# Attention scores of the last 64 rows of every head: made during the first batch, stored in DRAM and loaded again where their top 32 are searched

## The chip, the cores and the metric

One core of a Trainium2 chip runs the whole kernel. The metric is device time in microseconds (us) of one execution. Before the change three runs took 1207.24, 1211.10 and 1211.47 us, median 1211.1. The five engines of the core each work through their own list of instructions in order and wait for one another by semaphores: PE multiplies matrices, DVE (VectorE) searches the largest scores, ACT (ScalarE) copies and exponentiates, POOL (GpSimd) subtracts and scales, and SP issues all DMA transfers.

## The reference

Sparse attention and then two feed-forward layers (FFN), all in float32:

```python
B, H, S, D = 4, 8, 576, 64                      # q, k, v: (B, H, S, D)
scores = matmul(q, k^T) / sqrt(D)               # 576 x 576 for each of the 32 heads
kth    = the 32nd largest score of each row
attn   = softmax over the scores >= kth, 0 elsewhere
x      = matmul(attn, v)                        # heads side by side: 2304 tokens x 512
h = x @ moe_w_in;   x = max(0.01 * h, h) @ moe_w_out            # 512 -> 2048 -> 512
h = x @ moe2_w_in;  g = h where h >= 1, 0 where h <= -1, (h + 1)^2 / 4 between
out = g @ moe2_w_out
```

## The kernel before

**Units.** A head has 576 rows of queries, which is 4 x 128 + 64. The attention is cut into 80 units. A unit of kind "m" is 256 rows of one head: two tiles of 128 rows x 576 scores. There are 16 of them in each batch. A unit of kind "r" takes the last 64 rows of two neighbouring heads and stacks them into one tile of 128 rows, so that there are 4 in each batch and 16 in all. The r units do not run with their own batch: those of batches 0, 1 and 2 stand in batch 2 (`REMS`, line 32), and those of batch 3 in batch 3. So batch 0 and batch 1 have 16 units each, batch 2 has 28 and batch 3 has 20.

**A unit's path.** `st_scores` (line 720) loads the head's keys and queries and multiplies them on PE (`scores`, line 544). Except in the first eight heads ("plain", float32 products), every product is made of two float32r products: ACT casts the keys and the queries, POOL makes the remainders (`k_new`, `q_new`). Half a tile (288 columns) is made at a time, and ACT copies it from PSUM into a tile `s`, of which there are six. `topk` (line 571) then searches the 32 largest of each row on DVE with four MAX8 and three MATCH_REPLACE8 a tile, ACT and POOL make the probabilities `e`, PE transposes them and multiplies them with V (`pv`, `pv_pair`), and `split_x` makes the operands of the FFN.

**An r unit before.** It loads its queries from `qp`, where two heads' queries stand in columns of their own with zeros in the others', casts them, and takes both heads' keys. Where its batch is the one that runs, the keys are there already; otherwise both are loaded and split again. That is so in 8 of the 16 r units. Each half tile is then the sum of four float32r products (two heads x two parts), so an r unit has eight.

**The FFN.** A table (`FLOW`, line 36) says which blocks of rows go through which layer together. Its matmuls (`hidden`, `sums`, lines 818 to 873) have 512 columns, or 256 for the first rows of batch 0. Each product is again three float32r matmuls (lines 795 to 797, and 867 to 869). The weights come packed and are decoded once (`prep_w`, line 431: two operations of ACT, one of POOL and one of DVE, and a split by ACT and POOL), 64 tiles in all, during batches 0 and 1; they are written to DRAM (`scr`) and loaded later into six `ring` buffers. The FFN of batch 0 starts inside batch 0, with the weight tiles `px` as they come.

**What sets the order.** A planner (`Plan`, line 76) writes the instructions of all engines once, ahead of time, from assumed durations and a priority for each operation (the unit's number for attention, over 10000 for the FFN). What it has written is each engine's program; on the chip nothing overtakes. So PE's program is one fixed interleaving of attention and FFN, and SP's is one list of all the transfers.

## Time and profile before

| | |
|---|---|
| three runs | 1207.24, 1211.10, 1211.47 us |
| span of the profiled execution, first to last instruction | 1207.4 us |
| busy in it: PE, DVE, ACT, POOL | 1149.2, 876.4, 856.5, 742.6 us |
| bytes read from and written to DRAM | 187.5 and 38.3 MB |

The profiled execution's own time is not listed beside its span; a span of 1207.4 us puts it at the lower end of the three runs, 3.7 us (0.3%) under their median. A profile's busy time of PE counts each matmul with its way through the array, while the next already runs: a matmul of 512 columns shows 0.39 us though the next starts 0.23 us after it. So PE at 100% means that there was always one on its way, and how fast PE works is read from the starts of successive matmuls. PEclk is the granted TensorE clock as a share of 2.4 GHz; its two levels are 1.2 and 2.4 GHz.

### The profile page before, as it was taken

How to read it: one execution, taken by the hardware profiler on the slowest of the kernel's cores; microseconds unless marked ns; L12 is line 12 of the kernel's file. 1: busy time of each engine (PE TensorE's matmuls, PEld its weight loads, DVE VectorE, ACT ScalarE, POOL GpSimd, SP SyncE). 2: the span in 40 equal slices, each digit the busy share in tenths (PEclk: the TensorE clock that was granted, in tenths of full speed). 3: DMA queues.
4: the chain of work that ended last, by engine and by line, in shares of the span. 5: the costliest groups of instructions: out<-in, count | busy, mean ns of one | idle time of the engine just before them, and what ended most of it. 6: DMA issues, size and time to landing. Idle time of an engine off the chain costs nothing.

```text
span 1207.4 us, 18958 instructions
## 1 busy us (share of the span) xinstructions
PE 1149.2 (95%) x6304; PEld 979.6 (81%) x6304; DVE 876.4 (73%) x1759; ACT 856.5 (71%) x1921; POOL 742.6 (62%) x852
## 2 busy tenths in 40 slices
PE   5678987999999999999999999999999999999998
PEld 4457976998888888888888888888888888888886
DVE  7999999999999995998999999989981000012221
ACT  6788998998999898799989898987553211242222
POOL 2445786985988779697969578868563222242221
PEclk9788998999999999999999999999999999999999
DMA  9655985797557456655556454433445432333323
GB/s 318 201 193 192 352 323 185 254 349 274 207 215 250 171 178 197 204 184 185 184 194 225 160 194 151 140 128 122 140 157 178 154 130 99 121 140 140 127 103 103
DMA packets 71410, 227.02 MB, mean 188 GB/s; under 512 B 7952, under 2 KB 14224, under 8 KB 67216
## 3 DMA queue, kind: packets, MB, share of 16 engines
q1 hardware_dynamic: 71312, 225.80, 53.8%
q8 instruction: 50, 0.82, 0.3%
q14 instruction: 48, 0.39, 0.1%
HBM read 187.50 MB, written 38.27 MB: 187 GB/s over the span
## 4 chain that ended last, share of the span: by engine, by line
PE 79%; ACT 8%; POOL 5%; DVE 5%; issue 2%; DMA 1%; SPq 0%; POOLq 0%; ACTq 0%; DVEq 0%
PE bank L795 14%; PE bank L797 14%; PE bank L796 14%; PE bank L660 7%; PE bank L634 6%; PE bank L557 6%; PE bank L867 5%; PE bank L869 5%; PE bank L868 5%; DVE wk L584 2%; DVE m L580 2%; ACT e L602 2%; PE bank L680 2%; POOL px L381 1%; POOL e L619 1%
## 5 line engine op out<-in xcount | busy, mean ns | idle before, releaser
L381 POOL TENSOR_TENSOR gt<-gr,gt 128x512 fp32r<-128x512 f32 x144 | 189.0, 1313 | 235.2 <-ACT gt L365 115.6
L580 DVE MAX8 m<-wk 128x8 f32<-128x576 f32 x432 | 309.9, 747 | 1.1
L843 DVE TENSOR_SCALAR t<-bank 128x512 f32<-128x512 f32 x72 | 49.5, 687 | 240.0 <-PE bank L797 239.3
L584 DVE MATCH_REPLACE8 wk<-m,wk 128x576 f32<-128x576 f32 x288 | 212.4, 742 | 0.0
L795 PE MATMUL bank<-x,ring 128*128 128x512 f32 (+1 forms) x568 | 208.9, 368 | 0.2 <-DVE gr L846 0.2
L797 PE MATMUL bank<-x,ring 128*128 128x512 f32 (+1 forms) x568 | 203.3, 358 | 0.0
L796 PE MATMUL bank<-x,ring 128*128 128x512 f32 (+1 forms) x568 | 202.9, 357 | 0.0
L634 PE MATMUL bank<-idt,e 128*116 128x128 f32 (+1 forms) x720 | 114.4, 287 | 30.0 <-POOL e L619 26.0
L634 PEld LDWEIGHTS bank<-idt,e 128*116 128x116 f32 (+1 forms) x720 | 88.6, 141 | 52.5 <-POOL e L619 33.8
L580 DVE MAX8 m<-s 128x8 f32<-128x576 f32 x144 | 104.3, 746 | 31.4 <-ACT s L365 31.2
L365 ACT COPY s<-bank 128x288 f32<-128x288 f32 x288 | 106.5, 402 | 28.4 <-PE bank L557 27.0
L365 ACT COPY ptr<-bank 116x512 f32<-116x512 f32 (+1 forms) x224 | 107.3, 508 | 26.5 <-PE bank L634 25.7
L381 POOL TENSOR_TENSOR pt<-ptr,pt 116x512 fp32r<-116x512 f32 (+1 forms) x96 | 106.1, 1124 | 30.2 <-ACT pt L365 28.4
L797 PEld LDWEIGHTS bank<-x,ring 128*128 128x128 f32 x568 | 106.6, 188 | 17.4
L619 POOL TENSOR_SCALAR e<-e,rc 128x576 f32<-128x576 f32 x144 | 109.8, 772 | 16.5 <-DVE rc L617 14.4
L367 ACT ACTIVATE t<-t,half 128x512 f32<-128x512 f32 x72 | 52.0, 722 | 93.8 <-DVE t L843 93.7
L367 ACT ACTIVATE gt<-bank 128x512 fp32r<-128x512 f32 x72 | 43.2, 601 | 105.6 <-PE bank L797 105.4
L795 PEld LDWEIGHTS bank<-x,ring 128*128 128x128 f32 x568 | 106.9, 188 | 12.2 <-DVE gr L846 0.7
L796 PEld LDWEIGHTS bank<-x,ring 128*128 128x128 f32 x568 | 107.1, 189 | 11.2 <-POOL x L381 0.4
L795 PE MATMUL bank<-gt,ring 128*128 128x512 f32 (+1 forms) x304 | 110.4, 363 | 0.0
L367 ACT ACTIVATE e<-s,nb 128x576 f32<-128x576 f32 x144 | 108.9, 779 | 1.4
L557 PE MATMUL bank<-kk,qh 128*128 128x288 f32 x512 | 104.3, 310 | 4.3 <-ACT s L365 2.9
(92 smaller groups left out, 2875.6 us busy)
## 6 DMA issues: line engine op xcount, KB each, us to landing
ring<-scr SPq DMA_DIRECT2D x212, 512.0 KB, 3.5
scr<-px SPq DMA_DIRECT2D x58, 512.0 KB, 4.2
wraw<-in_moe_w_in_dram SPq DMA_DIRECT2D x16, 1024.0 KB, 6.1
wraw<-in_moe_w_out_dram SPq DMA_DIRECT2D x16, 1024.0 KB, 6.8
kraw<-in_km_dram SPq DMA_DIRECT2D x56, 288.0 KB, 3.9
vl<-in_vd_dram SPq DMA_DIRECT2D x24, 320.0 KB, 4.5
qraw<-in_qm_dram SPq DMA_DIRECT2D x24, 256.0 KB, 4.1
vl<-in_vp_dram SPq DMA_DIRECT2D x16, 320.0 KB, 3.8
```

Of the source, the lines that this page charges most:

```text
L365: nc.scalar.copy(out=out_(), in_=in_())
L367: nc.scalar.activation(out=out_(), in_=in_(), func=func, **a)
L381: lambda: nc.gpsimd.tensor_tensor(out=out_(), in0=in0(), in1=in1(), op=ALU.subtract),
L557: nc.tensor.matmul(ps()[:, 0:HALF], lhsT=qh()[:, at] if plain else qh()[:, part, at], rhs=kk()[:, c * HALF:(c + 1) * HALF], start=(i == 0) ...
L580: vec(lambda i=i, c=c, src=src: nc.vector.max(out=m()[:, i, c], in_=src()), 664, [(m, (i, r))], [src], pr)
L584: vec(lambda i=i, c=c, src=src, w=ws[i]: nc.vector.match_replace(out=w(), in_to_replace=m()[:, i, c], in_values=src(), imm_value=NEG), 720 ...
L619: P.op("P", T_NORM, lambda i=i: nc.gpsimd.tensor_scalar(out=es[i](), in0=es[i](), scalar1=rc()[:, i:i + 1], scalar2=1.0, op0=ALU.mult, op1 ...
L634: nc.tensor.transpose(ps()[0:p, i * 128:(i + 1) * 128], e()[:, cols[j]], idt())
L660: nc.tensor.matmul(out_ps()[:, 0:w], lhsT=vt()[0:p, j, :], rhs=pt()[0:p, c] if lean else pt()[0:p, part, c], start=bi == 0 and part == 0 a ...
L795: nc.tensor.matmul(ps, lhsT=wh, rhs=xh, start=first, stop=False, skip_group_check=True)
L796: nc.tensor.matmul(ps, lhsT=wh, rhs=xl, start=False, stop=False, skip_group_check=True)
L797: nc.tensor.matmul(ps, lhsT=wl, rhs=xh, start=False, stop=last, skip_group_check=True)
```

## The change

The scores of the r units are no longer made where they are used. During the first 16 units (batch 0), after each unit's own scores, `scores_kept` makes those of one r unit, in the order of `KEPT`: head pair 0 of batches 0 to 3, then head pair 1, and so on. The host lays out a new array `kp`: for each pair of heads and each half of the keys, 128 partitions that hold the first head's 64 dimensions above the second head's, with 288 columns of keys and behind them 128 columns of queries, where each head's 64 queries have zeros in the other head's partitions. One float32 product of 288 columns, contracted over all 128 partitions, is then a finished half tile for both heads. For each half there is a load of 208 KB, that product, a copy by ACT into a tile `t` and a store of 144 KB to DRAM. The loads go into buffers `gr` and `wa`, in turn. An r unit now only loads its 288 KB of scores into an `s` tile (`scores_again`) and its V. In the planner, the buffer for such a load has to be free for 2500 ns (`SLACK`) before the load is placed.

```diff
@@ -57,6 +57,9 @@
 NLEAN = 16
 NPLAIN = 8
 NSOFT = 72
+KEPT = tuple((b, c) for c in range(4) for b in (0, 1, 2, 3))
+HOMES = ("gr", "wa")
+PKEPT = (1.0, 1.0)
 FREE = (8.0, 14.0)
 
 
@@ -91,7 +94,7 @@
 
     def tile(self, tag, make, fifo=True, among=None):
         r = Ref(tag, make)
-        r.seq, r.fifo, r.among = None, tag if fifo is True else fifo, among
+        r.seq, r.fifo, r.among, r.loaded = None, tag if fifo is True else fifo, among, False
         return r
 
     def op(self, eng, ns, fn, w=(), r=(), prio=0.0, after=(), also=()):
@@ -149,6 +152,8 @@
             if ref.fifo and given.get(ref.fifo, 0) != ref.seq:
                 return None
             free = slots[ref.tag]
+            if ref.loaded:
+                free = {i: t + SLACK for i, t in free.items()}
             can = [i for i in (ref.among or free) if free.get(i, 1e18) <= now]
             return min(can, key=free.get) if can else None
 
@@ -230,8 +235,9 @@
                     if uses[ref] == 0 and ref.tag in self.bufs:
                         hop = HOP + (SLACK if ref.tag in LOADED else 0.0)
                         slots[ref.tag][ref.slot] = now + hop
-                        heapq.heappush(events, (now + hop, cnt, -1))
-                        cnt += 1
+                        for late in (0.0, SLACK):
+                            heapq.heappush(events, (now + hop + late, cnt, -1))
+                            cnt += 1
                 for j in succ[i]:
                     left[j] -= 1
                     e2 = self.ops[j][0]
@@ -279,8 +285,8 @@
     ctx: ExitStack,
     tc: tile.TileContext,
     qm: bass.AP,
-    qp: bass.AP,
     km: bass.AP,
+    kp: bass.AP,
     vm: bass.AP,
     vd: bass.AP,
     vp: bass.AP,
@@ -568,6 +574,31 @@
                 [(s, c)], [ps], pr)
         return s
 
+    def scores_kept(b, c, j, pr):
+
+        d = fixed([128, S], F32, f"s{b}_{c}", lambda: dram)
+        kept[b, c] = d
+        n = HALF + 2 * REM
+        for z in range(2):
+            kq = new(HOMES[j % len(HOMES)], [128, 512], fifo="keptk")
+            dma(lambda kq=kq, z=z: kq()[:, 0:n], lambda z=z: kp[b, c, z], n / 2, [kq], [], pr)
+            ps = bank(pr)
+            s = new("t", [128, 512], fifo="kept")
+            pe(lambda kq=kq, ps=ps: nc.tensor.matmul(
+                ps()[:, 0:HALF], lhsT=kq()[:, HALF:n], rhs=kq()[:, 0:HALF], start=True, stop=True),
+                4 * HALF / 2.4, [ps], [kq], pr, [s])
+            act(lambda s=s: s()[:, 0:HALF], lambda ps=ps: ps()[:, 0:HALF], t_a(HALF, True), [s], [ps], pr)
+            dma(lambda z=z: d()[:, z * HALF:(z + 1) * HALF], lambda s=s: s()[:, 0:HALF], 144, [(d, z)], [s], pr)
+
+    def scores_again(b, c, pr):
+
+        s = new("s", [128, S])
+        s.loaded = True
+        dma(s, kept[b, c], 288, [s], [kept[b, c]], pr)
+        return s
+
+    kept = {}
+
     def topk(tiles, soft, scale, pr):
 
         n = len(tiles)
@@ -732,10 +763,7 @@
             t0 = 2 * a if b in JOINT else 0
             return dict(u=u, tiles=[scores([(qh, t0 + t, kk)], pr, plain) for t in range(2)], v=vt,
                         scale=scale / 2 if plain else scale)
-        ks = [k_cur[b, 2 * h + e] if b == u_batch[0] else k_new(b, 2 * h + e, pr) for e in range(2)]
-        vt = v_pair(b, h, pr)
-        qh = q_new(lambda: qp[b, h], T, pr)
-        return dict(u=u, tiles=[scores([(qh, e, ks[e]) for e in range(2)], pr)], scale=scale, v=vt)
+        return dict(u=u, tiles=[scores_again(b, h, pr)], scale=scale, v=v_pair(b, h, pr))
 
     def second():
 
@@ -975,6 +1003,8 @@
             if i == 0:
                 made.add(0)
                 prep_layer(0)
+            if i < len(KEPT):
+                scores_kept(*KEPT[i], i, PKEPT[0] + PKEPT[1] * i)
             st[i]["es"] = topk(st[i]["tiles"], i < NSOFT, st[i]["scale"], float(i))
         if i >= AHEAD:
             unit_out(i - AHEAD)
@@ -999,13 +1029,14 @@
         return np.concatenate([a, a], axis=2)
 
     data.append(("qm", twice(q[:, :, :QM])))
-    qp = np.zeros((B, H // 2, 2 * D, 4 * REM), q.dtype)
-    last = twice(q[:, :, QM:])
+    data.append(("km", twice(k)))
+    half = S // 2
+    kp = np.zeros((B, H // 2, 2, 2 * D, half + 2 * REM), q.dtype)
     for e in range(2):
-        o = e * 128 + e * REM
-        qp[..., o:o + REM] = last[:, e::2]
-    data.append(("qp", qp))
-    data.append(("km", twice(k)))
+        kp[:, :, :, e * D:(e + 1) * D, :half] = k[:, e::2].reshape(B, H // 2, 2, half, D).transpose(0, 1, 2, 4, 3)
+        at = half + e * REM
+        kp[:, :, :, e * D:(e + 1) * D, at:at + REM] = q[:, e::2, None, QM:].transpose(0, 1, 2, 4, 3)
+    data.append(("kp", kp))
     nj = -(-S // KB)
     vp = np.zeros((B, H, nj * KB, D), v.dtype)
     vp[:, :, :S] = v
```

Names in the following rows: `kraw`, `qraw`, `vl`, `vraw` are loaded keys, queries and V; `wraw` is a packed weight; `idt` is the identity; `gr` and `wa` in the changed program hold the loaded `kp`; `bank` is PSUM; `s`, `t` and `x` are as above, and `s<number>_<number>` is the DRAM array of one kept r unit.

SP's list at the start of the program. Before, from the second packed weight on:

```order
L359 DMA wraw_151<-in_moe_w_in_dram 128x2048
L359 DMA vl_153<-in_vd_dram 128x640
L359 DMA kraw_155<-in_km_dram 128x576
L359 DMA qraw_157<-in_qm_dram 128x256
L359 DMA vl_161<-in_vd_dram 128x640
L359 DMA kraw_165<-in_km_dram 128x576
L359 DMA qraw_171<-in_qm_dram 128x256
```

Now, from the same transfer on:

```order
L365 DMA wraw_151<-in_moe_w_in_dram 128x2048
L365 DMA vl_153<-in_vd_dram 128x640
L365 DMA gr_155<-in_kp_dram 128x416
L365 DMA gr_157<-in_kp_dram 128x416
L365 DMA kraw_161<-in_km_dram 128x576
L365 DMA qraw_165<-in_qm_dram 128x256
L365 DMA vl_171<-in_vd_dram 128x640
L365 DMA wa_174<-in_kp_dram 128x416
L365 DMA wa_182<-in_kp_dram 128x416
L365 DMA kraw_187<-in_km_dram 128x576
L365 DMA qraw_189<-in_qm_dram 128x256
```

Two loads of `kp` now stand ahead of the second unit's keys and queries, and two more ahead of the third's.

PE's list behind the transposes of the tenth unit. Before (`L660` is the product with V, `L557` the next scores, `L795` and the two after it the FFN's hidden products):

```order
L660 MATMUL bank_222<-ptr_299,vl_161 128x256 x2
L660 MATMUL bank_222<-ptr_304,vl_161 128x256 x2
L660 MATMUL bank_222<-ptr_311,vl_161 128x256
L557 MATMUL bank_228<-kraw_155,qraw_157 128x288
L557 MATMUL bank_176<-kraw_155,qraw_157 128x288
L795 MATMUL bank_214<-x_437,ring_965 128x256
L796 MATMUL bank_214<-x_437,ring_965 128x256
L797 MATMUL bank_214<-x_437,ring_965 128x256
```

Now, at the same place (`L691` is the product with V, `L563` the scores, `L587` a kept product, `L665` the next unit's transposes):

```order
L691 MATMUL bank_169<-ptr_325,vl_171 128x256 x2
L691 MATMUL bank_169<-ptr_334,vl_171 128x256 x2
L691 MATMUL bank_169<-ptr_337,vl_171 128x256
L563 MATMUL bank_236<-kraw_161,qraw_165 128x288
L563 MATMUL bank_176<-kraw_161,qraw_165 128x288
L563 MATMUL bank_239<-kraw_161,qraw_165 128x288
L563 MATMUL bank_169<-kraw_161,qraw_165 128x288
L587 MATMUL bank_236<-wa_174 128x288
L665 MATMUL bank_176<-idt,e_252 116x128
```

A kept product stands between the scores and the next transposes, and the FFN's products that stood here come later in the list.

SP's list in batch 2, at a run of r units. Before:

```order
L359 DMA kraw_165<-in_km_dram 128x576
L359 DMA qraw_157<-in_qp_dram 128x256
L359 DMA ring_781<-scr0_5_1_1078 128x1024
L359 DMA ring_850<-scr0_8_0_908 128x1024
L359 DMA kraw_137<-in_km_dram 128x576
L359 DMA ring_965<-scr0_6_1_1204 128x1024
L359 DMA qraw_171<-in_qp_dram 128x256
```

Now, at the first run of them:

```order
L365 DMA ring_963<-scr0_5_0_574 128x1024
L365 DMA vraw_4238<-in_vm_dram 128x320
L365 DMA s_167<-s2_0_386 128x576
L365 DMA s_180<-s0_0_247 128x576
L365 DMA ring_1074<-scr0_3_1_921 128x1024
L365 DMA ring_702<-scr0_6_0_755 128x1024
L365 DMA vraw_4245<-in_vm_dram 128x320
L365 DMA s_241<-s1_0_331 128x576
```

The keys and queries of the r units are gone from here, and one load of scores stands for each. It waits for its `s` buffer, and loads of FFN weights (`ring`) stand behind it in the same list.

## Rows read from the trace of the kernel before

**Rows 1.** Page: the chain that ended last, share of the span by engine.

```profile
PE 79%; ACT 8%; POOL 5%; DVE 5%; issue 2%; DMA 1%; SPq 0%; POOLq 0%; ACTq 0%; DVEq 0%
```

**Rows 2.** Busy time by stretch; columns are named in the first line.

```profile
core 0: us, PE busy (x) PEld busy (x) DVE busy (x) ACT busy (x) POOL busy (x), PEclk, DMA share, GB/s
0.00:120.00 120.00, 84.07 (x357) 66.22 (x358) 109.72 (x234) 92.76 (x207) 53.66 (x77) 0.87 0.66 227
120.00:150.00 30.00, 30.00 (x211) 27.93 (x210) 29.56 (x60) 27.66 (x62) 22.11 (x28) 1.00 0.93 343
150.00:210.00 60.00, 48.46 (x275) 39.99 (x274) 57.88 (x113) 53.98 (x121) 43.44 (x50) 0.91 0.74 262
210.00:300.00 90.00, 85.12 (x626) 79.94 (x625) 85.23 (x173) 82.52 (x188) 72.32 (x82) 1.00 0.79 293
300.00:414.00 114.00, 113.84 (x552) 93.98 (x551) 111.86 (x205) 105.32 (x217) 97.04 (x101) 1.00 0.60 216
414.00:680.00 266.00, 266.00 (x1496) 228.04 (x1495) 238.36 (x502) 237.09 (x575) 216.67 (x263) 1.00 0.56 189
680.00:904.00 224.00, 223.37 (x1221) 188.74 (x1220) 205.08 (x422) 176.54 (x417) 155.75 (x184) 1.00 0.45 150
904.00:1207.00 303.00, 298.35 (x1580) 254.72 (x1579) 38.70 (x57) 80.61 (x144) 81.62 (x72) 1.00 0.37 129
```

**Rows 3.** DVE, in order of time: reciprocals of units 16, 32, 60 and 80.

```profile
198.53 0.17 DVE L617 RECIPROCAL rc<-rc 128x2 f32<-128x2 f32 x1 [0.80 <-POOL rc L615]
...
414.06 0.15 DVE L617 RECIPROCAL rc<-rc 128x2 f32<-128x2 f32 x1
...
680.65 0.15 DVE L617 RECIPROCAL rc<-rc 128x1 f32<-128x1 f32 x1
...
903.89 0.16 DVE L617 RECIPROCAL rc<-rc 128x1 f32<-128x1 f32 x1 [0.86 <-POOL rc L615]
```

**Rows 4.** PE in order of time: float32r score products amid the FFN.

```profile
507.35 0.70 PE L557 MATMUL bank<-kk,qh 128*128 128x288 f32 x4
507.88 0.28 PE L660 MATMUL bank<-pt,vv 112*128 112x256 f32 x1
```

**Rows 5.** PE in order of time: plain float32 score products, two records each.

```profile
4.09 4.18 PE L557 MATMUL bank<-kraw,qraw 128*128 128x288 f32 x8 [4.09 <-DMA qraw<-in_qm_dram]
...
63.11 2.10 PE L557 MATMUL bank<-kraw,qraw 128*128 128x288 f32 x8
```

**Rows 6.** Waits of PE from 0 to 210 us: sum, times, longest.

```profile
PE bank L634 <- POOL e L619: 25.3, 21, 3.5
```

**Rows 7.** Groups by line: busy, mean ns, idle before.

```profile
L365 ACT COPY s<-bank 128x288 f32<-128x288 f32 x288 | 106.5, 402 | 28.4 <-PE bank L557 27.0
...
L381 POOL TENSOR_TENSOR px<-wb,px 128x512 fp32r<-128x512 f32 x58 | 76.3, 1320 | 25.2 <-ACT px L365 23.3 <-PE bank L660 1.5
```

**Rows 8.** The start in order of time, on PE, ACT and DVE.

```profile
13.81 7.69 PE L557 MATMUL bank<-kraw,qraw 128*128 128x288 f32 x24 [5.54 <-DMA qraw<-in_qm_dram]
...
16.11 0.40 ACT L365 COPY s<-bank 128x288 f32<-128x288 f32 x1 [0.56 <-PE bank L557]
...
18.20 1.41 DVE L580 MAX8 m<-s 128x8 f32<-128x576 f32 x2
```

**Rows 9.** DMA issues: count, KB each, median us to landing.

```profile
kraw<-in_km_dram SPq DMA_DIRECT2D x56, 288.0 KB, 3.9
...
out_dram<-t SPq DMA_DIRECT2D x16, 256.0 KB, 4.0
```

**Rows 10.** Waits of the DMA queue, whole span: sum, times, longest.

```profile
SPq L359 <- PE bank L797: 390.4, 126, 12.9
```

**Rows 11.** Waits of DVE from 414 to 904 us: sum, times, longest.

```profile
DVE m L580 <- ACT s L365: 25.0, 15, 7.3
DVE rc L617 <- POOL rc L615: 8.2, 18, 0.9
DVE t L843 <- PE bank L797: 7.8, 13, 1.3
DVE gr L846 <- ACT t L367: 2.5, 6, 0.8
```

## The prediction

> **What bounds the kernel now.** I read the chain of waits first: PE holds 79% of it, ACT 8%, DVE 5% [rows 1]. That is a mean over stages with different limits, so the busy times by stretch come next [rows 2], cut at DVE's reciprocals of units 16, 32, 60 and 80, which close batches 0 to 3 at 198.5, 414.1, 680.7 and 903.9 us [rows 3].
>
> In batch 0 DVE sets the pace. From 0 to 210 us it is busy for 197.2 us (109.72 + 29.56 + 57.88), PE for 162.5 (84.07 + 30.00 + 48.46). PE's idle time is thus 47.5 us, and 25.3 us of it is waiting for POOL's scaled probabilities [rows 6], which come from DVE's search: PE has time there. From 210 to 300 us PE still idles 4.9 us. From 300 us to the end of attention it idles 0.8 us in 604; the FFN always has a matmul left. Behind 904 us PE works alone for 303 us on what the FFN has not yet done. So from 300 us on a microsecond less on PE is a microsecond less in the end, if the attention can follow: DVE is busy 443.4 of the 490 us of batches 2 and 3 (90.5%), and 25.0 us of its waits there are for score tiles, which PE makes between FFN products [rows 11].
>
> Is PE really full there? Its weight loads fill 228.04 of 266 us (85.7%) in batch 2, against 254.72 of 303 (84%) in the tail, where nothing but its own matmuls holds it back. So I take it as full; rival 5 is the other case.
>
> **Removed, on the path.** Each of 16 r units had eight float32r products of 288 columns. Four of them take 0.53 us from the first start to the start of what follows [rows 4], so 0.1325 each: 16 x 8 x 0.1325 = 17.0 us of PE, 12 units of it in batch 2 and 4 in batch 3. Value -17.0. With it go casts of ACT and subtractions of POOL for 16 key tiles and 16 query tiles, and 32 copies of 0.402 us by ACT [rows 7]; neither engine bounds these batches (237.1 and 216.7 of 266 us), so I count nothing.
>
> **Added on PE, in batch 0.** 32 float32 products. Eight records of such products, two for each, take 2.10 us [rows 5]; less the 0.41 us that the last one shows by itself, that is 0.241 a record and 0.48 a product, 15.4 us in all. At the lower clock of the start (4.18 us for eight) it is 0.96, and 31 us if all ran so. All 32 stand in PE's list ahead of the transposes of the 17th unit, in the time in which PE idles 47.5 us. They hide behind DVE: 0. Should half of them stand in DVE's way, it is 7.7.
>
> The Trainium skill, FP8 and Floating Point Precision, section TensorE Precision Notes, says that a true float32 product takes four passes of the array. By it one kept half costs the same as the four float32r products that it replaces, and the change saves no PE work at all; the two records of 0.241 us agree to 10%. The rows say the same without it: 17.0 us go, 15.4 come, and the gain stands or falls with PE's idle time in batch 0. A rival below rests on that.
>
> **Added on ACT.** 32 copies from PSUM like those of the score tiles, 0.402 us each: 12.9 us, in batch 0, where ACT is busy 174.4 of 210 us. It rises to 89%. DVE hardly waits for ACT there after the start, as the tiles are made up to three units ahead; but ACT is also on the way from search to transposes. From 0 to 12.9; I take 1, near the lower end, as six score tiles lie between.
>
> **Added on SP and the DMA engines.** 64 transfers of 208 and 144 KB, 11.5 MB, in some 160 us. Nearest rows: 288 KB lands in 3.9 us, a store of 256 KB in 4.0 [rows 9]. That is 72 GB/s more on top of 227; the same engines carry 343 from 120 to 150 us. The start is where it shows: two loads (0.43 MB) now go ahead of the second unit's keys. Before, its products start at 13.81 us, after a wait for that load [rows 8], by which 3.3 MB had come, so 0.43 MB are 1.5 to 1.8 us. Its first score tile was whole at 16.5 us and DVE took it at 18.20, so the first tile just keeps its place and the second comes about 1.5 us late. Value 1.5, bounds 0 and 4.
>
> **Moved: the FFN in batch 0.** Counting PE's list, 558 FFN products of 256 columns stand ahead of the 18th unit's transposes before and 420 now. At 0.12 us each that is 16.6 us of PE work put off, because the weight tiles come later: DVE has done 26 weight operations by its 16th unit, where it had done 30. By the 25th unit the list is ahead instead (768 + 90 of 512 columns against 768 + 30, 14 us), and by the 33rd level (393 against 396). PE must fit that into 150 to 300 us, where it idled 11.5 + 4.9 us. It just fits: value 0, bounds -5 and +17.
>
> **Moved: the r units' scores.** A load of 288 KB needs 3.9 us. The six `s` tiles go round in a fixed order, and in batch 2 a tile lasts 266 / 44 = 6 us, so four tiles' time, 24 us, lies between the freeing of a buffer and its next use. What is queued behind the waiting load on SP are FFN weights for PE, but there SP waits for PE's free buffers anyway (390.4 us, 126 times [rows 10]): 0.
>
> **Can DVE follow?** The attention of batches 2 and 3 would shrink from 490 us by 17.0, and by 7 more, since PE's list now leaves 30 FFN products of 512 columns (7 us) more to the tail. DVE then has 443.4 us of work in 466, 95%. From 300 to 414 us it did 111.86 of 114 (98%) with PE full. So it can, with some friction: 2, bounds 0 and 15.
>
> **Sum.** -17.0 + 0 + 1 + 1.5 + 0 + 2 = -12.5 against the profiled span of 1207.4: 1194.9. The runs' median lies 3.7 us above that span, and I carry this over: 1198.6.
>
> **Rivals.**
> 1. *DVE takes over in batches 2 and 3.* If its 25.0 us of waits for score tiles stay, because m units' tiles still queue behind FFN products, it needs 443.4 + 25.0 + 8.2 + 7.8 + 2.5 = 486.9 of 490 us, the attention saves 3 us and PE idles in the rest. Against it: these waits are PE's lack of time, which shrinks. -3 + 1.5: about 1209.5.
> 2. *PE's idle time in batch 0 is no use*, because it comes in short gaps that end with probabilities. Then each kept product delays a transpose and that unit's FFN, 15.4 us come back, and what is left is -1.6: 1209.5. For it: 25.3 us of idle in 21 pieces of at most 3.5 us. Against: DVE does not wait for transposes.
> 3. *The weights come too late* (slower). In batch 0 the packed weights stand in one SP list with 64 more transfers, and ACT, which unpacks them, has 12.9 us more. PE then idles the 16.6 us of FFN put off, and has to do them when POOL, which makes the weights' and the FFN's remainders (1.32 us a tile [rows 7]), is busy 72.3 of 90 us. It decides from where more than 14 us of the 16.6 are lost: 17 + 1.5 + 1 + 2 - 17.0 = +4.5, and with four late weight tiles and three FFN steps on POOL (about 12 us) +16: 1216 to 1227, middle 1220. Against: the list catches up within seven units.
> 4. *More than the sum.* The packed list from unit 18 to 25 also fills gaps that PE had from 150 to 300 us (16.4 us); half of it and no friction give -24: 1187.
> 5. *PE only looks full in batches 2 and 3*, since a matmul's record runs on while the next has begun. Then the removed products leave gaps behind and nothing ends earlier: 1211.1 + 1.5 = 1212.6. For it: weight loads fill only 85.7% of batch 2 [rows 2]. Against: they fill no more of the tail, 84%, where PE waits for nothing but itself. The Trainium skill, Perfetto Trace Analysis, section Identifying the Most-Contended Engine, has this as its rule: matmul busy time does not tell how close PE is to its limit, the share of weight loads does. By it PE would have some 14% to spare in batch 2; the tail, which has the same share, speaks against reading it so here.
>
> That the change does not do what it says is ruled out by the lists: 448 scores products instead of 576, and 16 loads of scores.
>
> **Chances.** The forecast 0.57 (own range 1193 to 1204), rival 1 0.11, rival 2 0.09, rival 3 0.14, rival 4 0.06, rival 5 0.03. Runs of this kernel differ by 4 us, so 0.5%, 6 us, is about what can be told from no change. Faster by more: the forecast, rival 4 and a little of rivals 1 and 2, 0.66. Slower by more: most of rival 3, 0.12. The same: 0.22. A range of 1190 to 1212 leaves out half of rival 4, most of rival 3 and a little of the forecast's edges, 0.2.
>
> **What would show it.** The reciprocal of unit 16 within 3 us of 198.5: the kept work hides. That of unit 32 within 5 of 414: the put-off FFN fitted (rival 3: later by 15). From there to the last one some 468 us instead of 490, with DVE at 95% (rival 1: 487). PE's idle time up to 300 us 52.4 - 15.4 = 37 us instead of 52.4 (rival 2: no less). The tail some 7 us longer than 303. I am wrong if batch 1 ends after 425 us, or if DVE's waits in batches 2 and 3 stay at their 43.5 us or grow.

## The result and the profile after

The changed kernel takes 1191.06 us (median of four runs, 1190.79 to 1191.56) against 1211.28 for the kernel before (1207.24 to 1211.84): ratio 0.9838, 95% interval 0.9826 to 0.985. That is 20.2 us less by the medians and 18.4 by the profiled spans (1207.4 and 1189.0). The forecast was 12.5 by the spans and a time of 1198.6, in a range of 1190 to 1212. (A run's time lies 1.7 to 1.9 us above its own span in every run on record. The execution profiled before, with a span of 1207.4, thus took some 1209.2 us; it was not at the lower end of the runs but amid them.)

The chain of waits first: PE still holds most of it, two points less than before [rows 1].

```profile
PE 77%; ACT 7%; DVE 6%; POOL 6%; issue 2%; DMA 1%; SPq 0%; POOLq 0%; ACTq 0%; DVEq 0%
```

Then DVE's reciprocals of units 16, 32, 60 and 80 in the changed kernel, which answer to [rows 3]; the first column is the start.

```profile
193.83 0.15 DVE L648 RECIPROCAL rc<-rc 128x2 f32<-128x2 f32 x1
...
413.89 0.17 DVE L648 RECIPROCAL rc<-rc 128x2 f32<-128x2 f32 x1 [0.20 <-POOL rc L646]
...
667.80 0.16 DVE L648 RECIPROCAL rc<-rc 128x1 f32<-128x1 f32 x1 [0.46 <-POOL rc L646]
...
879.83 0.16 DVE L648 RECIPROCAL rc<-rc 128x1 f32<-128x1 f32 x1 [0.51 <-POOL rc L646]
```

Batch 0 ends 4.7 us earlier and batch 1 at the same time (413.9 and 414.1). Batches 2 and 3 take 465.9 us instead of 489.8, and what remains takes 309.2 instead of 303.5. So all of the gain is made behind unit 32: 793.3 us before, 775.1 now.

Busy time by stretch of the changed kernel, cut at its own milestones; the columns are those of [rows 2].

```profile
core 0: us, PE busy (x) PEld busy (x) DVE busy (x) ACT busy (x) POOL busy (x), PEclk, DMA share, GB/s
0.00:120.00 120.00, 89.06 (x374) 67.81 (x375) 110.11 (x234) 99.00 (x229) 51.77 (x77) 0.89 0.87 303
120.00:150.00 30.00, 25.51 (x146) 20.49 (x145) 29.83 (x62) 25.79 (x64) 17.51 (x23) 1.00 0.74 243
150.00:210.00 60.00, 54.48 (x391) 50.30 (x390) 58.98 (x117) 58.54 (x129) 51.27 (x56) 1.00 0.92 339
210.00:300.00 90.00, 85.69 (x624) 80.33 (x624) 81.65 (x166) 81.91 (x184) 72.02 (x82) 1.00 0.83 305
300.00:414.00 114.00, 113.16 (x557) 93.30 (x556) 112.31 (x209) 108.44 (x225) 98.61 (x102) 1.00 0.64 222
414.00:668.00 254.00, 253.83 (x1399) 214.94 (x1397) 240.19 (x506) 218.83 (x527) 185.07 (x235) 1.00 0.55 184
668.00:880.00 212.00, 212.00 (x1157) 179.33 (x1156) 196.87 (x414) 168.19 (x393) 149.65 (x176) 1.00 0.48 155
880.00:1189.00 309.00, 304.26 (x1607) 259.66 (x1605) 40.03 (x58) 81.87 (x146) 83.07 (x73) 1.00 0.37 130
```

PE is still full from 300 us on, in less time. In batches 2 and 3 DVE is busy 437.1 of 466 us (94%; before 90.5%). The DMA engines carry 303 GB/s in the first 120 us, where it was 227. The DMA issues of the kept work, with the size of each transfer and the median time to landing:

```profile
s<-t SPq DMA_DIRECT2D x32, 144.0 KB, 4.8
s<-s SPq DMA_DIRECT2D x16, 288.0 KB, 4.1
...
gr<-in_kp_dram SPq DMA_DIRECT2D x16, 208.0 KB, 6.1
wa<-in_kp_dram SPq DMA_DIRECT2D x16, 208.0 KB, 4.2
```

DVE's waits in batches 2 and 3 now, answering to [rows 11]: sum, times, longest.

```profile
DVE rc L648 <- POOL rc L646: 16.1, 27, 1.2
DVE t L871 <- PE bank L825: 7.2, 13, 1.7
DVE m L611 <- ACT s L371: 2.4, 2, 2.0
DVE gr L874 <- ACT t L373: 1.1, 2, 0.8
```

The wait for score tiles has gone from 25.0 us to 2.4; all four together from 43.5 [rows 11] to 26.8.

### The profile page after: what moved, and what is told of

It reads as the page before. It is cut to its first block, busy times and chain, and to the rows that moved or that the text cites. A ratio compares the mean times of both kernels' runs of the same rounds, so it can differ in the third digit from the quotient of the medians.

```text
span 1189.0 us, 18887 instructions
## 1 busy us (share of the span) xinstructions
PE 1138.0 (96%) x6240; PEld 966.2 (81%) x6240; DVE 870.0 (73%) x1759; ACT 842.6 (71%) x1889; POOL 709.0 (60%) x820
## 4 chain that ended last, share of the span: by engine, by line
PE 77%; ACT 7%; DVE 6%; POOL 6%; issue 2%; DMA 1%; SPq 0%; POOLq 0%; ACTq 0%; DVEq 0%
PE bank L823 15%; PE bank L825 15%; PE bank L824 15%; PE bank L691 6%; PE bank L665 5%; PE bank L895 5%; PE bank L897 5%; PE bank L896 5%; PE bank L563 4%; DVE m L611 3%; DVE wk L615 2%; PE bank L711 2%; POOL px L387 1%; ACT e L633 1%; POOL wb L460 1%
## 5 line engine op out<-in xcount | busy, mean ns | idle before, releaser
L665 PE MATMUL bank<-idt,e 128*116 128x128 f32 (+1 forms) x720 | 111.2, 282 | 16.4 <-POOL e L650 9.7
L665 PEld LDWEIGHTS bank<-idt,e 128*116 128x116 f32 (+1 forms) x720 | 86.6, 139 | 40.0 <-POOL e L650 16.0
L823 PE MATMUL bank<-gt,ring 128*128 128x512 f32 (+1 forms) x304 | 109.9, 361 | 0.0
L371 ACT COPY s<-bank 128x288 f32<-128x288 f32 x256 | 95.9, 402 | 17.9 <-PE bank L563 16.6
L825 PE MATMUL bank<-gt,ring 128*128 128x512 f32 (+1 forms) x304 | 107.1, 352 | 0.0
```

Of the source, the lines that this page charges most:

```text
L371: nc.scalar.copy(out=out_(), in_=in_())
L665: nc.tensor.transpose(ps()[0:p, i * 128:(i + 1) * 128], e()[:, cols[j]], idt())
L823: nc.tensor.matmul(ps, lhsT=wh, rhs=xh, start=first, stop=False, skip_group_check=True)
L825: nc.tensor.matmul(ps, lhsT=wl, rhs=xh, start=False, stop=last, skip_group_check=True)
```

## The experiments

The theory to test is that of the prediction: the change takes hardly any work from PE (17.0 us out, 15.4 in). It moves work from where PE sets the end to where PE waits anyway. The rivals were that the gain comes from relieving ACT and POOL of the casts, from the new order of the lists, from a higher granted clock, or that PE has room in batches 2 and 3. Every run falls into the same columns, of its profiled execution: how long until unit 32's reciprocal, how much of that from 112 us on PE was granted the lower clock (summed over half-microsecond stretches; before 112 us every kernel has 17 to 48 us of it), and how long from unit 32 to the end. The medians are of runs in five groups, in which the kernel before took 1211.28, 1209.59, 1210.18, 1209.63 and 1211.34 us.

| kernel | to unit 32, us | of it at the lower clock | from there to the end | median of the runs |
|---|---|---|---|---|
| before | 414.1 | 10.2 | 793.3 | 1211.28 |
| changed | 413.9 | 0 | 775.1 | 1191.06 |
| kept products made twice | 421.4 | 10.2 | 775.0 | 1194.51 |
| kept work left out | 419.4 | 13.7 | 775.0 | 1196.38 |
| left out, PE given stand-ins | 418.2 | 10.2 | 775.1 | 1194.75 |
| spare products at the r units | 413.6 | 0 | 790.1 | 1207.16 |
| spare products in batch 1 | 426.2 | 0 | 776.3 | 1208.09 |
| kept work begun later | 429.4 | 20.5 | 774.1 | 1204.53 |
| kept work begun sooner | 431.2 | 20.5 | 776.4 | 1204.82 |
| kept work in batch 1 | 456.1 | 27.3 | 773.6 | 1231.53 |
| stacked products in place | 416.1 | 3.4 | 793.8 | 1209.77 |
| casts back | 419.4 | 0 | 771.6 | 1193.85 |
| before, one of four products | 413.9 | 10.2 | 788.0 | 1205.54 |
| the same, list laid anew | 413.5 | 3.4 | 784.1 | 1199.91 |

The time behind unit 32 is 772 to 776 us in every kernel that has no products of that kind at the r units, and 790 to 794 in the three that have 15 to 17 us of them there (before, spare products, in place). Two of the equal times are not equally good: with the kept work in batch 1 and with it begun later, PE had by unit 32 done 46 and 37 FFN products of 512 columns more than in the changed kernel (two of 256 counted as one), some 10.6 and 8.5 us that were no longer left to do. What the move cost stands in the first column, and there the kernels differ by 42 us.

The first three columns are of one execution each. For the spare products it is one of the fastest of its kernel's runs (1205.47 and 1204.30 us), for the kept products made twice, the products in place and the work begun later and sooner it is the slowest (1198.14, 1211.69, 1205.29 and 1209.43).

That a higher granted clock makes the gain is ruled out by the runs' mean clock, a share of 2.4 GHz: it is 0.988 in every run of the changed kernel and mostly 0.979 to 0.986 in those of the kernel before, whose runs at 0.986 still took 1209.2 to 1209.8 us.

**One of four products, in the kernel before.** Of each r half tile's four products only the first is made; the lists stay as they were.

```diff
                     for part in range(parts):
+                        if len(pairs) > 1 and i > 0:
+                            continue
...
-                            stop=(i == n - 1),
+                            stop=(i == n - 1 or len(pairs) > 1),
```

> The kernel before, with all its lists, but each half tile of an r unit is made by one float32r product instead of four (three of the four are left out of the computation); loads, casts, copies and buffers stay. Theory: the change's gain is PE time taken out of batches 2 and 3, where PE is always full, so 96 products x 0.1325 = 12.7 us less: 1198.6, between 1196 and 1201. Rival, relief: the gain comes from the dropped casts of ACT, subtractions of POOL and loads, which all stay here: 1209 to 1212.

Measured: 1205.54 us (1203.43 to 1206.31), ratio 0.9958 (0.9942 to 0.9973), against 1209.59 for the kernel before on that chip. 4 us by the medians, 5.5 by the spans, of 12.7 taken out. Two stretches of its table, behind units 32 and 60, and DVE's longest wait in them:

```profile
414.00:677.00 263.00, 261.31 (x1427) 217.58 (x1426) 238.71 (x504) 236.73 (x576) 216.11 (x263) 1.00 0.57 191
677.00:898.00 221.00, 220.20 (x1191) 184.38 (x1190) 203.94 (x419) 175.67 (x414) 155.60 (x182) 1.00 0.46 151
```

```profile
DVE m L582 <- ACT s L365: 23.5, 13, 7.0
```

PE looks as full as before, but its weight loads fall to 82.7% of batch 2 (217.58 of 263), where they were 85.7% [rows 2]. I summed the time from each matmul's start to the next one's between units 32 and 80: 10.8 us less at score products, 5.4 more at others, about half of it at FFN products that stand ahead of a transpose or a score product. So in a fixed list half of the time that is taken from PE comes back as short waits, and DVE goes on waiting 23.5 us for score tiles. In this, rival 5 was partly true: PE's full column hid such waits.

**The same, with the planner told.** Its assumed duration for these products is cut to one quarter, so the lists are laid anew.

```diff
-            pe(mm, n * (4 * HALF / 2.4 if plain else t_m(HALF)), ...
+            pe(mm, (1 if len(pairs) > 1 else n) * (4 * HALF / 2.4 if plain else t_m(HALF)), ...
```

> As the run in which one product of four was left of each r half tile of the kernel before (three left out of the computation; it moved by 4 us of 12.7), but the planner is told the shorter duration and lays all lists anew. Theory A, the fixed list kept the rest, waits stood where the list was laid for longer products: 1197 to 1200. Theory B, the rest needs the relief of ACT and POOL (casts and subtractions of the r units' keys and queries): 1204 to 1208.

Measured: 1199.91 us (1199.46 to 1202.55), ratio 0.992 (0.9904 to 0.9936): 10.3 of the 12.7. Its attention ends no earlier (unit 80 at 904.6 us), but the tail is 293 us where it was 303.5: the planner filled the time with FFN products. By the spans it is 9.7. What is freed on PE thus counts by some four fifths here, if the order is laid anew for it; in the changed kernel it was. This is one new list, and the last two runs below show how far lists can differ ahead of unit 32; but 9.2 of the 9.7 us come behind it.

**Work put back at the r units.** Two spare plain products of 288 columns at each r unit's transposes, 32 in all, 15.4 us of PE; the lists of the changed kernel stay.

```diff
         def tr():
+            for _ in range(2 if len(es) == 1 and js[0] == 0 else 0):
+                nc.tensor.matmul(ps()[:, 0:HALF], lhsT=idt(), rhs=es[0]()[:, 0:HALF], start=True, stop=True)
```

> The changed kernel with two spare float32 products of 288 columns (identity times the unit's probabilities, overwritten at once) ahead of each r unit's transposes: 32 x 0.48 = 15.4 us of PE work put back in batches 2 and 3, the lists otherwise the same. Theory: PE time there counts one to one: 1206.5, between 1203 and 1208. Rival, relief of ACT, POOL and SP: 1191 to 1193. Rival, DVE now bounds those batches (95% busy) and hides part of it: 1196 to 1201.

Measured: 1207.16 us (1205.47 to 1211.36), ratio 0.9981 (0.9965 to 0.9997): 16.1 us above the changed kernel (14.7 by the spans). Batches 2 and 3 of this run:

```profile
414.00:677.00 263.00, 262.87 (x1433) 221.58 (x1432) 239.85 (x503) 218.56 (x525) 184.63 (x235) 1.00 0.53 177
677.00:893.00 216.00, 216.00 (x1177) 182.88 (x1175) 197.16 (x414) 168.95 (x392) 149.35 (x176) 1.00 0.46 152
```

Added work counts about one to one there: 9.6 us more in batch 2, 4.3 in batch 3. PE is the bound of these batches.

**The kept products made twice, in batch 0.** Another 32 plain products, right behind the kept ones; same lists.

```diff
-            pe(lambda kq=kq, ps=ps: nc.tensor.matmul(
-                ps()[:, 0:HALF], lhsT=kq()[:, HALF:n], rhs=kq()[:, 0:HALF], start=True, stop=True),
+            pe(lambda kq=kq, ps=ps: [nc.tensor.matmul(
+                ps()[:, 0:HALF], lhsT=kq()[:, HALF:n], rhs=kq()[:, 0:HALF], start=True, stop=True) for _ in range(2)],
```

> The changed kernel, with every kept float32 product issued twice into the same bank, 32 products (15.4 us at the full clock) more in batch 0, nothing else moved in any list. Theory: they hide in PE's idle time behind DVE: 1191 to 1194. Rival, the kept work costs its PE time (the change would have gained more without it): 1200 to 1207. The same rival in half: 1197.

Measured: 1194.51 us (1193.02 to 1198.14), ratio 0.987 (0.9838 to 0.9902): 3.4 us for 15.4 of PE work (7.4 by the spans, in its slowest run, with 10.2 us at the lower clock that the changed kernel hasn't). Products of this size cost 15 to 16 us at the r units and 3 to 7 here. That is the effect of the place by itself.

**The kept work left out.** No loads, products, copies and stores of it, in the lists of the changed kernel; an r unit loads 288 KB of keys in place of its scores.

```diff
...
-            pe(lambda kq=kq, ps=ps: nc.tensor.matmul(
-                ps()[:, 0:HALF], lhsT=kq()[:, HALF:n], rhs=kq()[:, 0:HALF], start=True, stop=True),
+            pe(lambda: None,
...
-        dma(s, kept[b, c], 288, [s], [kept[b, c]], pr)
+        dma(s, lambda: km[b, c], 288, [s], [kept[b, c]], pr)
```

> The changed kernel with the loads, products, copies and stores of the kept scores left out of the lists and all else in its place; the r units load a head's keys instead of their scores, so the output is not the reference's. It prices the whole added work of batch 0. Theory: it is nearly free, 1 to 3 us: 1188 to 1190. Rival, the added work costs its PE time: 1176. Rival, its transfers and ACT copies cost while its products do not: 1180 to 1186.

Measured: 1196.38 us (1195.89 to 1197.75), ratio 0.9884 (0.9851 to 0.9917). Without the added work the kernel is 5 us slower, which none of my theories had. From unit 32 on the two kernels run alike (775.0 and 775.1), so it is lost ahead of it. The granted clock shows a difference there: three stretches of this kernel, each at the lower level (1.2 GHz) almost throughout, and then the changed kernel's from 104 us to unit 32.

```profile
126.00:132.80 6.80, 6.08 (x20) 5.25 (x21) 6.71 (x13) 3.75 (x8) 0.87 (x2) 0.52 0.13 52
204.40:207.80 3.40, 3.40 (x11) 2.79 (x10) 3.40 (x8) 2.70 (x6) 2.50 (x2) 0.52 0.92 323
286.30:289.70 3.40, 3.40 (x17) 3.40 (x18) 3.40 (x8) 2.56 (x5) 3.32 (x3) 0.52 0.95 377
```

```profile
104.00:194.00 90.00, 81.45 (x519) 70.23 (x518) 87.62 (x180) 83.31 (x191) 63.78 (x74) 1.00 0.87 309
194.00:414.00 220.00, 210.58 (x1261) 184.06 (x1260) 209.64 (x402) 205.65 (x440) 183.95 (x198) 1.00 0.72 259
```

13.7 us at half the clock are at most 6.8 us of PE's work, enough for the 5.5 by which unit 32 is late. So the kept work costs next to nothing in this list, as forecast: without it, and with the clock kept up, the kernel would be at most 6.8 - 5.5 = 1.3 us faster. Whether it is the kept products that hold the clock up, the next run asks.

**Left out, with stand-ins for PE.** As above, but each kept product is replaced by two small ones of 128 columns on the identity, which wait for no load, so that PE has something to do at these points.

```diff
-            pe(lambda: None,
+            pe(lambda ps=ps: [nc.tensor.matmul(
+                ps()[:, 0:128], lhsT=idt(), rhs=idt(), start=True, stop=True) for _ in range(2)],
```

> The changed kernel with the kept scores' loads, copies and stores left out, as in the run that was 5 us slower, but with a stand-in in the place of each kept product: two float32 products of 128 columns of the identity with itself, 0.43 us, which wait for nothing (the r units load keys instead of their scores, so the output is not the reference's). Theory, that run was slower because PE, with less to do in batch 0, was granted the lower clock in batch 1 more often: 1188 to 1192. Rival, it was slower for another reason, such as the order in which transfers land: 1194 to 1198.

Measured: 1194.75 us (1193.87 to 1195.66), ratio 0.9871 (0.9857 to 0.9886): only 1.6 us better than left out. Unit 16 now comes at 194.4 us, as in the changed kernel, but behind it the clock falls all the same. The same 5 us of the two kernels, the stand-ins' first and the changed one's second:

```profile
200.00:205.00 5.00, 4.51 (x12) 3.57 (x13) 4.67 (x9) 3.77 (x9) 3.59 (x4) 0.50 0.75 250
```

```profile
200.00:205.00 5.00, 4.79 (x28) 3.94 (x29) 5.00 (x10) 4.95 (x12) 3.27 (x4) 1.00 0.86 273
```

12 matmuls against 28, at half the clock, though both kernels had just made the same wait; again the stand-ins' kernel first:

```profile
200.49 0.68 PE L665 MATMUL bank<-idt,e 128*112 128x128 f32 x2 [3.12 <-ACT ptr L371]
```

```profile
199.96 0.43 PE L665 MATMUL bank<-idt,e 128*112 128x128 f32 x2 [3.09 <-ACT ptr L371]
```

So the loss and the lower clock go together in both kernels without kept work (and 10.2 us of it can hold the 4.3 us by which unit 32 is late here), but that PE only needs something to do at these points is refuted. Over all their runs, the mean granted clock of the four kernels with these lists rises with PE's work in batch 0: 0.978 to 0.983 with the kept work left out, 0.984 to 0.986 with the stand-ins, 0.988 in the changed kernel, 0.989 to 0.996 with the kept products made twice. Why the same wait goes with the lower level in one kernel and not in the other stays open.

**Spare products in batch 1.** As at the r units, but at 16 units of batch 1.

```diff
+            for _ in range(2 if 16 <= pr < 32 and js[0] == 0 else 0):
+                nc.tensor.matmul(ps()[:, 0:HALF], lhsT=idt(), rhs=es[0]()[:, 0:HALF], start=True, stop=True)
```

> The changed kernel with two spare float32 products of 288 columns (overwritten at once) ahead of the transposes of each of the 16 units of batch 1: 15.4 us of PE work, all lists otherwise the same. It tells what PE time costs in batch 1 without the fight for key buffers of the run that made the kept scores there. Theory, PE and DVE are both about full in batch 1: 10 to 16 us more, 1201 to 1207. Rival, batch 1 has room and that run lost its time to key buffers: 1191 to 1195.

Measured: 1208.09 us (1203.22 to 1209.88), ratio 0.9983 (0.997 to 0.9996): 17.0 above the changed kernel, and 13.5 by the spans, of a faster run: about one to one. In batch 1 PE has no time to spare either, although DVE is busy over 95% of it.

**The kept work in batch 1.** Begun 16 units later; its loads go through the key buffers, since `gr` and `wa` are in use by then.

```diff
...
-            if i < len(KEPT):
-                scores_kept(*KEPT[i], i, PKEPT[0] + PKEPT[1] * i)
+            if 16 <= i < 16 + len(KEPT):
+                scores_kept(*KEPT[i - 16], i, 1.0 + i)
```

> The change with the kept scores made during the 16 units of batch 1 instead of batch 0 (their loads go into key buffers, since the FFN uses gr there). Theory, they were free because PE has idle time in batch 0, and in batch 1 PE and DVE are both about full: most of 15.4 us comes back, 1201 to 1208. Rival, they are free anywhere ahead of the r units: 1190 to 1195.

Measured: 1231.53 us (1229.65 to 1232.74), ratio 1.0175 (1.016 to 1.0191). Dearer than its 15.4 us by far: batch 1 takes 261 us instead of 220. Its stretch and DVE's two longest waits in it:

```profile
195.00:456.00 261.00, 242.18 (x1328) 205.81 (x1326) 211.06 (x403) 214.96 (x465) 179.69 (x196) 0.96 0.71 250
```

```profile
DVE m L611 <- ACT s L371: 15.7, 4, 8.0
DVE rc L648 <- POOL rc L646: 14.1, 5, 5.7
```

The sign is as expected, the size is not: score tiles come late where the kept loads hold key buffers, and the clock is lower. How much belongs to each was not taken apart.

**The stacked product in place.** Each r unit loads its part of `kp` and makes its two plain products itself; nothing is stored. All lists are laid anew.

```diff
...
-        return dict(u=u, tiles=[scores_again(b, h, pr)], scale=scale, v=v_pair(b, h, pr))
+        return dict(u=u, tiles=[scores_here(b, h, pr)], scale=scale, v=v_pair(b, h, pr))
...
```

> The stacked plain products of the change, but made where the r units stand: each loads its two halves of kp and multiplies there; nothing is stored, batch 0 has no added work, the casts, subtractions and key loads of the r units are gone as in the change. PE does 15.4 us in place of 17.0 in batches 2 and 3. Theory, PE time there is what counts: 1.6 us less than before and a list laid anew: 1205 to 1211. Rival, relief of ACT, POOL and SP makes the gain: 1191 to 1196. Both, half each: about 1201.

Measured: 1209.77 us (1207.94 to 1211.69), ratio 0.9994 (0.9985 to 1.0003). All casts and subtractions that the change saves, and the r units' loads of queries and keys, are saved here too, and nothing is gained. The products' new form is worth nothing in this list without their new place.

**The casts back.** The changed kernel, with the r units' queries, and in 8 of 16 both heads' keys, loaded, cast and split again, unused.

```diff
+        if b != u_batch[0]:
+            for e in range(2):
+                k_new(b, 2 * h + e, pr)
+        q_new(lambda: qm[b, 2 * h][:, 0:T], T, pr)
```

> The changed kernel with the loads, casts and subtractions of the r units' keys and queries put back in batches 2 and 3 (nothing reads what they make; queries from another array of the same shape), lists laid anew. Theory A, PE time alone: 1190 to 1194. Theory B, their absence is a third or more of the gain: 1197 to 1204.

Measured: 1193.85 us (1192.77 to 1194.99), ratio 0.9869 (0.9852 to 0.9885): 2.8 us above the changed kernel. ACT's and POOL's relief is at most a small part. (Unit 32 comes 5.5 us later in this list, but 13 FFN products of 512 columns, 3.0 us, had moved ahead of it, and 3.5 us come back behind it.)

**Begun later, begun sooner.** The only edit is the priority of the kept work, by which the planner lays other lists with the same work in them: `PKEPT` of (3.0, 0.8) and of (0.0, 0.9) instead of (1.0, 1.0).

> The change with the kept scores given priorities 3.0 + 0.8 i instead of 1.0 + 1.0 i, so that no load of kp stands ahead of the second and third units' keys; lists laid anew. If the start costs the change what the second unit shows (its reciprocal 2 us later than before), 1189 to 1190. If batch 0 absorbs that anyway: 1190 to 1194.

> The changed kernel with the kept work's priorities set 1.0 to 2.5 units earlier (0.0 + 0.9 x i instead of 1.0 + 1.0 x i), so that it ends in batch 0 with more room; all lists are laid anew by the planner, and no work is added or taken out. If only the place of the PE work counts, it stays within 4 us of the changed kernel, 1187 to 1195, since all of it still lies in batch 0. If the planner's list of the day counts for as much as the run with the later begin suggests (13 us worse with the same work), it may come out anywhere from 1183 to 1207, and outside 1187 to 1195 more likely than within; the difference then shows in batches 1 and 2, not in batch 0.

Measured: 1204.53 us (1200.94 to 1205.29), ratio 0.9946 (0.9929 to 0.9963), and 1204.82 (1203.54 to 1209.43), ratio 0.9944 (0.9927 to 0.996). Both miss the numbers of the theory of place by some 10 us. Of the other expectations, the one for the later run missed too; for the sooner run the wide span held, but not the place, since it loses 11.8 us in batch 0 and 5.5 in batch 1. Batches 0 and 1 of the run begun sooner:

```profile
0.00:205.60 205.60, 169.05 (x836) 138.82 (x836) 183.53 (x381) 170.93 (x388) 110.25 (x141) 0.88 0.83 297
205.60:431.20 225.60, 216.21 (x1256) 186.60 (x1257) 211.66 (x406) 204.71 (x441) 184.37 (x196) 0.98 0.69 249
```

DVE has the same work there as in the changed kernel (395 and 393 us), but 36 us of idle time instead of 21, and the granted clock is lower in both batches (in those of the changed kernel it is 0.93 and 1.00). The clock is not the main cause: another run of this list had a mean clock of 0.987, where the changed kernel has 0.988, and took 1204.72 us. Nor is it more work: by unit 32 PE has done four FFN products of 512 columns more than in the changed kernel. In the list begun later it has done 37 more, 8.5 us, so there about half of the loss lies behind unit 32, which should have been shorter by as much. What the two lists lose it by was not taken apart.

So the 17 us of products that are gone behind unit 32 belong to the change, and that nothing was paid for them elsewhere belongs to this list: two neighbours of it ended some 14 us later, not far from what 15.4 us of products would cost on the path, as in rival 2; the trace doesn't say that it was they. No version beats the changed kernel.

## Why the prediction was right, and where it was off

The forecast's mechanism held; its size did not in full. 1191.06 us lies inside the stated range but 2 us below the 1193 to 1204 that the forecast had for itself. And luck is in it: three lists with this work in batch 0 took 1191, 1204.5 and 1204.8 us, and no term of the sum tells which of them the planner would lay.

- **Removed, 17.0 us of PE in batches 2 and 3: right.** From each one's start to the next matmul's, the score products between units 32 and 80 take 51.0 us before and 34.0 now. 18.2 us went behind unit 32, with 23.9 in the batches (forecast: 22) and 5.7 given back in the tail (7). The runs with work put back (+16.1) and with one of four products in a new list (-10.3 of 12.7) show that PE's time is what counts there. The step left out a condition, that the order is laid anew: in the old lists 4 to 5.5 of 12.7 come.
- **Added on PE, hidden in batch 0: right for this list,** with a gain on the clock beside it that I had not seen: the kernel before spent 10.2 us at the lower level between 112 us and unit 32, up to 5 us of PE's work, and the changed one none. Up to that much the kept work may have cost. (That products at the start run at the lower clock, the prediction read from their doubled time; the trace has no granted clock for the first 17 us.) Unit 16 came at 193.8, 1.7 us outside the forecast's 3 us around 198.5, on the early side. Two rows of DVE's weight operations up to unit 16, before and after, account for it: count, busy time, mean.

```profile
L460 DVE SCALAR_TENSOR_TENSOR wb<-wa,wb 128x512 int32<-128x512 int32 x14 | 15.4, 1117 | 0.7 <-ACT wb L367 0.4
```

```profile
L466 DVE SCALAR_TENSOR_TENSOR wb<-wa,wb 128x512 int32<-128x512 int32 x10 | 9.7, 984 | 0.1
```

  Four operations (5.7 us) had moved to batch 1. I had counted them (26 and 30), but only for what PE gets late, not for what DVE gets early.
- **The FFN put off fits by unit 32: right.** 413.9 us, forecast 414 within 5; rival 3 is out in this list. PE had then done ten FFN products of 512 columns fewer (2.3 us) and a unit's transposes and products with V more. In the two neighbours unit 32 came at 429.4 and 431.2, which is rival 3's 15 us late; that late weights were the reason is not shown.
- **The three small costs, 4.5 us: terms that were mis-sized.** ACT 1 and the start 1.5 were to show in batches 0 and 1, which took 0.2 us less in all. PE did wait 4.8 us for the first kept load at 12.79 us, and the second unit's reciprocal came at 35.39 instead of 33.39; but the third came at 42.95 instead of 43.90, so the start's delay was absorbed within one unit. DVE's friction of 2 did not come, since its waits for score tiles nearly vanished. With 1.3 us less given back in the tail, that is the 5.9 us between -12.5 and -18.4 (2.7 + 1.9 + 1.3). The other 1.6 us to the median are the distance of median from span, carried over as 3.7 and now 2.1; 1.8 of each is what a run takes beyond its span, and the rest was chance: the execution profiled before was some 2 us faster than the median.
- **PE's idle time up to 300 us: missed.** Forecast 37, measured 45.3 (before 52.4). The kept products take 19.6 us of the busy column and the FFN 3.3 more than before, but the attention's other matmuls, nearly as many, take 15.9 us less. From 17 us on, where both traces have the granted clock, PE was busy at the lower level for 37.1 us before and 16.8 now, which is up to 10 us of that. The forecast had taken the clock as the same in both. PE's waits for probabilities fell from 25.3 us [rows 6] to 9.0, and others came:

```profile
PE bank L665 <- POOL e L650: 9.0, 12, 4.2
PE bank L563 <- ACT t L371: 5.8, 4, 3.1
PE bank L587 <- DMA gr<-in_kp_dram: 4.8, 1, 4.8
```

- **The rivals.** Rival 1 is out: DVE's waits fell to 26.8 us. Rival 2's full price is out here (a second set of kept products cost 3.4, by the spans 7.4). Rival 4's size came close (1187), but not by its mechanism: PE's idle time from 150 to 300 us did fall, from 16.4 us to 9.8, yet unit 32 came no earlier. Rival 5 is out for added work and half true for removed work.

What stays open is how much a given list will cost ahead of unit 32. The lists differ there by up to 17 us with the same kept work, as much as the largest term of my sum, and the forecast gave that no term.

## What to carry to other kernels

Ask of a change that trades work on one engine for as much work elsewhere in time, where that engine sets the end and where it waits; here 15 us of such products cost 14 to 17 us where it sets the end and 3 to 7 where it waits. In an order laid out ahead of time, what is taken out may pay by less than half (4 of 12.7 us) until the order is laid anew (10.3), while what is added where the engine is full costs about in full at once. And where a planner lays it, run two or three neighbouring settings before crediting the edit with the whole difference: of the 20 us here, some 14 were lost again by the order alone.

## What the runs showed of the hardware that I had not expected

Leaving work out made the kernel 5 us slower, with the granted clock at its lower level for 13.7 us between 112 us and unit 32; kernels with nearly the same list had 0 to 10.2 us of it. The same wait of PE for `ptr`, 3.09 and 3.12 us long, went with a granted clock of 1.00 in the changed kernel and of 0.50 in the one with stand-ins. The loads of 208 KB into `gr` and `wa` landed in 6.1 and 4.2 us (medians of 16 each), longer than the 3.9 us of 288 KB before [rows 9], beside 303 GB/s of traffic in the first 120 us; the third unit ended no later for it.
